# Attention followed by two MLP layers on one core: a third buffer for decoded weights, and the static instruction order drawn again

## The chip, the core and the metric

The kernel runs on one core of one Trainium2 chip. The metric is device time in microseconds (us) of one execution, the median of several runs. Five engines work side by side, each on its own queue in order: TensorE (PE, with its weight loads shown as PEld), VectorE (DVE), ScalarE (ACT), GpSimd (POOL) and SyncE (SP), which here only starts DMAs.

## What is computed

The reference, cut to what matters:

```python
# q, k, v: 4 batches, 8 heads, 576 positions, 64 wide
scores = q @ k.transpose(0, 1, 3, 2) / sqrt(64)
thresh = max(scores, axis=-1) - tau                 # tau = 0.02
scores = where(scores >= thresh, scores, -1e9)
attn   = exp(scores - max(scores));  attn /= sum(attn) + 1e-9
x      = (attn @ v) as 2304 tokens of 512
h  = x @ w_in;    x = (h * cos(h)) @ w_out          # 512 -> 2048 -> 512
h  = x @ w_in2;   out = (s * relu(h)**2 + b) @ w_out2
```

The weights arrive as 64-bit numbers, and the kernel decodes them to 32 bits itself.

## The kernel before

**Attention.** The work is cut into 16 pairs of heads (`pair(n)`), and a pair into nine tiles of 128 rows. A tile goes through: `scores` on PE (L312) into one of two PSUM tiles `s`; `stat` on DVE (L330), the row minimum `mn` of the negated scores; `limit` on POOL (the threshold `thr`); `expo` on ACT (L338, `e`); and `mask` on DVE (L342, `p`, with row sums), which also frees the `s` tile. `turn` (L271) transposes finished tiles on PE into PSUM tiles `pt`, and ACT copies them to `PT`. `weighted` (L425) multiplies with `v` in ten pieces for a pair (`av`), `finish` copies the result out on ACT, and `normalise` scales it on POOL.

**Layers.** 2304 tokens go through in five blocks for each of two layers, four of 512 tokens and one of 256. A block has 16 steps `f` (`step`; two at a time in the small block): `hidden` on PE (L651, 12 matmuls into `h`), an activation of five or seven instructions on DVE, ACT and POOL that ends with `gl` on POOL, and `output` on PE (L749, 12 matmuls into `acc`). The float32 factors are split in a high and a low part and multiplied in three products.

**Decoding.** Each layer has 32 half-weights: for each `f` a half of `w_in` and one of `w_out`. `decode` (L520) loads a raw tile `wr` by DMA (ring of two), then makes the word in a tile `wt` (ring of two): `magnitude` on ACT, `clamp` on POOL, `shift`, `sign` and `fill` on DVE (L545, L550, L555; `fill` frees `wr`), then `high` on ACT, or on POOL for the first 15 halves, and `low` on POOL, which frees `wt`. The first 15 halves of layer 1 have memory of their own and are decoded in the attention's time; the other 17 must wait until the attention's tiles are given up. Layer 2's halves take the places of layer 1's.

**The order.** Nothing of the order is left to a compiler. Class `Order` collects every operation with its engine, a planned length in ns, a rank, what it comes after, and the ring places that it takes and gives back. `run` (L80) plays the plan in planned time: on each engine it looks at the first 48 operations by rank, finds the one that could start first, and takes the lowest rank among those that could start within `SLACK` ns of it. `LAG`, 90 ns, is put between engines, and `tail` is time after an operation's end before its result counts. The operations are then issued in that order, and each engine keeps to it whatever the real times are. A rank is a place such as `base = n * PAIR` for pair n, `at = base + i * PAIR // 9` for tile i, or `close + step * STEP` in the layers, plus an offset from the table `PLACE`. Ranks only say which operation goes first; `PAIR` needn't be the time of a pair.

Of the kernel before, what the change touches and what calls it, by code (L numbers as in the profile page):

```python
# [27 lines left out]
class Order:  # L28
# [3 lines left out]

    SLACK = 262
    LAG = 90
    WINDOW = 48

# [12 lines left out]
    def add(self, engine, length, rank, fn, after=(), take=(), give=(), tail=0):  # L51
        op = dict(
            n=len(self.ops), engine=engine, length=length, rank=rank, fn=fn,
            after=[a for a in after if a is not None], take=tuple(take), give=tuple(give),
            tail=tail, start=None, end=None,
        )
        self.ops.append(op)
        return op
# [57 lines left out]
EARLY = 15  # L116

WEIGH = (3, 4)
PAIR = 16840

PLACE = {
    "scores": -6086, "stat": -3181, "exp": -7313, "mask": 1993, "turn": 1108, "turned": 3152, "rest": 443,
    "rested": -1757, "sums": 1929, "weigh0": -252, "weigh1": 4687, "weigh_step": 1086, "finish": -4708,
    "normalise": 40063, "keys": -30127, "early": 3.337, "early_step": 1.142, "first": 3.121, "second": 1.354,
    "second_step": 0.963, "first_step": 0.523, "xin": -10749, "active": 5021, "output": 5748,
}
STEP = 5450

# [2 lines left out]
def attention_moe_moe2_kernel(  # L131
# [33 lines left out]
    add, ring, ticket = order.add, order.ring, order.ticket  # L165
# [32 lines left out]

    for half in halves[:EARLY]:
        open_w(half)  # L200
    wtp = ctx.enter_context(tc.tile_pool(name="wtp", bufs=2))
    mg = ctx.enter_context(tc.tile_pool(name="mg", bufs=2))


# [13 lines left out]

    for name, size in (
        ("s", 2), ("pt", 4), ("q", 2), ("k", 1), ("ks", 2), ("v", 2), ("e", 2), ("p", 12), ("PT", 2),  # L220
        ("rb", 1), ("xs", 1), ("wr", 2), ("wt", 2), ("r", 2), ("gh", 2), ("gl", 2), ("mn", 6), ("thr", 6),
    ):
        ring(name, size)

# [3 lines left out]
    mixed = 4  # L228
# [4 lines left out]
    def pair(n):  # L233
# [3 lines left out]
        tk = {x: ticket(x) for x in ("q", "k", "ks", "v", "PT", "rb", "xs")}  # L237
# [18 lines left out]
        lk, lq, lv = load("k"), load("q"), load("v")  # L256
# [9 lines left out]
        ks = add("POOL" if n else "ACT", 700, base + PLACE["keys"], scale_keys, after=[lk], take=[tk["ks"]], give=[tk["k"]])  # L266
# [4 lines left out]
        def turn(tiles):  # L271
            if "PT" not in T:
                T["PT"] = apt.tile([P, 9, S], F32, tag="PT", name=f"PT{n}")
            pts = T["pt", tiles[0]] = [ps_t.tile([P, 512], F32, tag="pt", name=f"pt{n}_{tiles[0]}_{g}") for g in range(2)]
            for k in range(4):
                for j, i in enumerate(tiles):
                    p = T["p", i].rearrange("p a b -> p (a b)")
                    for g in range(2):
                        o = slice(64 * g, 64 * g + 64)
                        c = (k * len(tiles) + j) * 64  # L280
                        nc.tensor.transpose(pts[g][:, c : c + 64], p[o, k * 128 : k * 128 + 128], ident[o, o])  # L281
            if tiles[0] == mixed:
                p = T["p", mixed].rearrange("p a b -> p (a b)")
                nc.tensor.transpose(pts[0][0:64, 256:320], p[0:64, 512:S], ident[0:64, 0:64])
                nc.tensor.transpose(pts[1][:, 256:320], p[64:128, S - 128 : S], ident[64:128, 64:128])
# [16 lines left out]
        masks, scored, transposed = [], [], []  # L302
        ptk = []
        for i in range(9):
            for _ in range(WEIGH.count(i)):
                yield
            at = base + i * PAIR // 9
            heads = [0] if i < mixed else [1] if i > mixed else [0, 1]
            ts, te, tp, tm, th = ticket("s"), ticket("e"), ticket("p"), ticket("mn"), ticket("thr")
            ptk.append(tp)  # L310

            def scores(i=i):  # L312
                st = T["s", i] = ps_s.tile([P, 2, 512], F32, tag="s", name=f"s{n}_{i}")
                for h in range(2):
                    g = slice(64 * h, 64 * h + 64)
                    if i != mixed:
                        c, hd = columns[i], int(i > mixed)
                        nc.tensor.matmul(  # L318
                            st[:, h, :H2], T["q"][g, c : c + 128], T["ks"][g, hd * H2 : (hd + 1) * H2],
                            start=True, stop=True,  # L320
                        )
                        continue
                    for hd in range(2):
                        c = 512 + 64 * hd
                        nc.tensor.matmul(  # L325
                            st[64 * hd : 64 * hd + 64, h, :H2], T["q"][g, c : c + 64], T["ks"][g, hd * H2 : (hd + 1) * H2],
                            start=True, stop=True,
                        )

            def stat(i=i):  # L330
                T["mn", i] = atiny.tile([P, 1], F32, tag="mn", name=f"mn{n}_{i}")
                nc.vector.tensor_reduce(out=T["mn", i], in_=T["s", i][:, :, :H2], axis=mybir.AxisListType.XY, op=ALU.min)  # L332

            def limit(i=i):
                T["thr", i] = atiny.tile([P, 1], F32, tag="thr", name=f"thr{n}_{i}")
                nc.gpsimd.tensor_tensor(out=T["thr", i], in0=T["mn", i], in1=ptau, op=ALU.add)  # L336

            def expo(i=i):  # L338
                T["e", i] = ape.tile([P, 2, H2], F32, tag="e", name=f"e{n}_{i}")
                nc.scalar.activation(T["e", i], T["s", i][:, :, :H2], AF.Exp, bias=T["mn", i], scale=-1.0)  # L340

            def mask(i=i):  # L342
                if "sm" not in T:
                    tail_ops()
                p = T["p", i] = app.tile([P, 2, H2], F32, tag="p", name=f"p{n}_{i}")
                nc.vector.scalar_tensor_tensor(  # L346
                    out=p, in0=T["s", i][:, :, :H2], scalar=T["thr", i], in1=T["e", i], op0=ALU.is_le, op1=ALU.mult,
                    accum_out=T["sm"][:, i : i + 1],
                )

            s_ = add("PE", 600 if i == mixed else 500, at + PLACE["scores"], scores, after=[lq, ks] if i == 0 else [], take=[ts],
                     give=[tk["q"], tk["ks"]] if i == 8 else [], tail=250)
            scored.append(s_)
            m_ = add("DVE", 755, at + PLACE["stat"], stat, after=[s_], take=[tm])
            t_ = add("POOL", 190, at + PLACE["stat"], limit, after=[m_], take=[th])
            e_ = add("ACT", 735, at + PLACE["exp"], expo, after=[m_], take=[te], give=[tm])
            k_ = add("DVE", 890, at + PLACE["mask"], mask, after=[e_, t_], take=[tp], give=[ts, te, th])
            masks.append(k_)
            if i in (1, 3, 4, 6, 8):
                tiles = [i] if i == mixed else [i - 1, i]  # L360
                tt = [ticket("pt"), ticket("pt")]
                r_ = add("PE", 280 * len(tiles), at + PLACE["turn"], lambda t=tiles: turn(t), after=[masks[j] for j in tiles],
                         take=[*tt, *([tk["PT"]] if i == 1 else [])], tail=170)
                for g in (1, 0):
                    c_ = add("ACT", 170 + 215 * len(tiles), at + PLACE["turned"], lambda g=g, t=tiles: store_turned(g, t),
                             after=[r_], give=[tt[g]])
                    transposed.append(c_)
        end = base + PAIR

# [19 lines left out]
        r_ = add("PE", 650, end + PLACE["rest"], turn_rest, after=masks, take=tt, give=ptk, tail=170)  # L389
# [52 lines left out]
        for h in range(2):  # L442
            yield
            ts = ticket("pt")
            for k in range(5):
                v1 = add(
                    "PE", 490 + 100 * (k % 4 == 0), end + PLACE[f"weigh{h}"] + k * PLACE["weigh_step"], lambda h=h, k=k: weighted(h, k),
                    after=[*transposed, lv] if h == k == 0 else [v1], take=[ts] if k == 0 else [],
                    give=[tk["PT"], tk["v"]] if h * k == 4 else [],
                    tail=250 * (k == 4),  # L450
# [3 lines left out]
                take=[tk["xs"]] if h == 0 else [], give=[ts],  # L454
# [65 lines left out]
    def decode(half, rank, opened):  # L520
# [52 lines left out]
        early = opened is None  # L573
        o = add("SP", 60, rank - 6000, load, take=[tr], tail=4000)
        o = add("ACT", 675, rank, magnitude, after=[o], take=[tt])
        o = add("POOL", 620 if early else 720, rank, clamp, after=[o])
        o = add("DVE", 430 if early else 600, rank, shift, after=[o])
        o = add("DVE", 690 if early else 1030, rank, sign, after=[o])
        o = add("DVE", 690 if early else 1150, rank, fill, after=[o], give=[tr])
        o = add("POOL" if early else "ACT", 630, rank, high, after=[o, opened], take=[tw])  # L580
        o = add("POOL", 1270 if early else 1370, rank, low, after=[o], give=[tt])
# [302 lines left out]
```

## Time and profile before

| what | value |
|---|---|
| three runs | 1146.82, 1147.77, 1151.14 us; median 1147.77 us |
| profiled execution | 1150.11 us, its span 1148.3 us |
| PE busy | 1075.1 us (94% of the span) |
| DVE busy | 657.6 us (57%) |
| ACT busy | 483.7 us (42%) |
| POOL busy | 455.2 us (40%) |

The profiled execution is 2.3 us above the median, and its span leaves 1.8 us of it outside. The shares are means over stages with different limits: the attention up to some 313 us, layer 1 with decoding beside it, layer 1 alone, layer 1's end and layer 2's start with layer 2's decoding beside them, and layer 2 alone. [...]

### The profile page before, as it was taken

To read this page: it belongs to the slowest core of one execution; us is meant where nothing else is said; L and a number is where in the kernel's file an instruction comes from. 1 tells how busy PE (TensorE), PEld (TensorE's weight loads), DVE (VectorE), ACT (ScalarE), POOL (GpSimd) and SP (SyncE) were. 2 spreads that over 40 slices of the span, in tenths; PEclk is the share of its full clock that TensorE was granted. 3 is DMA by queue.
4 is the path that set the end of the run, shared out by engine and by line. 5 is a ranking of instruction groups with operands and counts; after the bars stand their busy time and mean duration, and the time that the engine had idled before them with its cause. 6 is when DMAs were issued, how large, how long until landed. Compare 5 with 4: busy or idle time off the path is not lost.

```text
span 1148.3 us, 17581 instructions
## 1 busy us (share of the span) xinstructions
PE 1075.1 (94%) x6736; PEld 816.2 (71%) x6736; DVE 657.6 (57%) x1062; ACT 483.7 (42%) x880; POOL 455.2 (40%) x556
## 2 busy tenths in 40 slices
PE   5988897889799889999999999999999999999998
PEld 3544444444467657889988877788888898888886
DVE  5778888788888864344553677887821222112211
ACT  4767776667644342222322343454422222223221
POOL 1133424233377744333333466676632222222222
PEclk9989999999899989999999999999999999999999
DMA  4232423232132211000010012333200000000100
GB/s 163 65 115 79 137 83 133 83 115 73 60 103 92 91 57 36 1 1 1 1 37 1 19 58 87 95 91 93 74 37 1 1 37 1 19 1 1 37 1 37
DMA packets 23507, 63.59 MB, mean 55 GB/s; under 512 B 4464, under 2 KB 4736, under 8 KB 23424
## 3 DMA queue, kind: packets, MB, share of 16 engines
q1 hardware_dynamic: 23280, 62.48, 16.8%
q8 instruction: 53, 0.87, 0.3%
q14 instruction: 30, 0.25, 0.1%
q10 hardware_dynamic: 144, 0.00, 0.0%
HBM read 57.67 MB, written 4.79 MB: 54 GB/s over the span
## 4 chain that ended last, share of the span: by engine, by line
PE 70%; DVE 14%; issue 7%; POOL 5%; ACT 2%; DMA 1%; POOLq 0%; DVEq 0%; ACTq 0%; SPq 0%
PE h L657 27%; PE acc L760 14%; PE acc L758 12%; PE s L318 7%; PE av L430 6%; DVE wt L550 3%; PE pt L281 2%; DVE p L346 2%; DVE wt L555 2%; DVE wt L545 2%; DVE mn L332 2%; DVE r L687 1%; POOL r L700 1%; PE s L325 1%; POOL wt L542 1%
## 5 line engine op out<-in xcount | busy, mean ns | idle before, releaser
L657 PE MATMUL h<-x,wh 128*128 128x512 f32 (+1 forms) x1280 | 371.2, 375 | 8.3 <-DVE r L708 6.3
L189 POOL TENSOR_TENSOR gl<-r,gh 128x512 fp32r<-128x512 f32 x144 | 190.8, 1325 | 306.5 <-DVE gh L731 242.1
L657 PEld LDWEIGHTS h<-x,wh 128*128 128x128 f32 x1280 | 232.3, 189 | 59.4 <-DVE r L708 9.4
L657 PE MATMUL h<-x,wl 128*128 128x512 f32 (+1 forms) x640 | 239.4, 374 | 0.3 <-POOL wl L189 0.3
L687 DVE TENSOR_SCALAR r<-r,s_t,b_t 128x512 f32<-128x512 f32 x72 | 44.0, 613 | 191.5 <-ACT r L226 191.5
L318 PE MATMUL s<-ks,q 64*128 64x288 f32 x512 | 108.4, 500 | 47.4 <-DVE p L346 35.0
L226 ACT ACTIVATE r<-h 128x512 f32<-128x512 f32 x72 | 43.2, 599 | 232.8 <-PE h L657 215.9
L657 PEld LDWEIGHTS h<-x,wl 128*128 128x128 f32 x640 | 120.8, 189 | 23.9 <-POOL wl L189 0.9
L332 DVE TENSOR_REDUCE mn<-s 128x1 f32<-128x576 f32 x144 | 108.9, 756 | 46.0 <-PE s L318 39.7
L340 ACT ACTIVATE e<-s,mn 128x576 f32<-128x576 f32 x144 | 106.5, 739 | 51.2 <-DVE mn L332 49.1
L346 DVE SCALAR_TENSOR_TENSOR p<-s,thr,e 128x576 f32<-128x576 f32 x144 | 116.2, 814 | 14.4 <-ACT e L340 10.0
L758 PE MATMUL acc<-gh,wh 128*128 128x512 f32 (+1 forms) x320 | 119.1, 372 | 4.0 <-ACT wh L568 4.0
L758 PE MATMUL acc<-gl,wh 128*128 128x512 f32 (+1 forms) x320 | 119.2, 372 | 2.6 <-POOL gl L189 2.6
L226 ACT ACTIVATE r<-r,hpi 128x512 f32<-128x512 f32 x72 | 51.9, 721 | 163.8 <-POOL r L700 163.6
L758 PE MATMUL acc<-gh,wl 128*128 128x512 f32 (+1 forms) x320 | 119.2, 372 | 0.1
L760 PE MATMUL acc<-wh,gl 128*128 128x512 f32 x288 | 112.6, 391 | 0.0
L760 PE MATMUL acc<-wl,gh 128*128 128x512 f32 x288 | 112.4, 390 | 0.0
L760 PE MATMUL acc<-wh,gh 128*128 128x512 f32 x288 | 112.3, 390 | 0.0
L318 PEld LDWEIGHTS s<-ks,q 64*128 64x128 f32 x512 | 45.8, 208 | 86.2 <-issue 52.4
L189 POOL TENSOR_TENSOR wl<-wt,wh 128x512 fp32r<-128x512 f32 x64 | 89.9, 1405 | 39.5 <-ACT wh L568 38.8
L336 POOL TENSOR_TENSOR thr<-mn,ptau 128x1 f32<-128x1 f32 x144 | 32.4, 227 | 176.5 <-DVE mn L332 170.8
L430 PE MATMUL av<-PT,v 128*64 128x288 f32 x640 | 96.2, 420 | 0.0
(64 smaller groups left out, 1436.5 us busy)
## 6 DMA issues: line engine op xcount, KB each, us to landing
wr<-in_w_dram SPq DMA_DIRECT2D x64, 512.0 KB, 3.6
q<-in_qt_dram SPq DMA_DIRECT2D x15, 576.0 KB, 3.8
v<-in_va_dram SPq DMA_DIRECT2D x16, 320.0 KB, 3.6
k<-in_kt_dram SPq DMA_DIRECT2D x16, 288.0 KB
out_dram<-ob SPq DMA_DIRECT2D x18, 256.0 KB, 2.2
rb<-rd SPq DMA_DIRECT2D x16, 144.0 KB, 3.4
rb<-rd SPq DMA_DIRECT2D x16, 128.0 KB, 3.1
q<-in_qt_dram SPq DMA_DIRECT2D x1, 448.0 KB
```

Of the source, the lines that this page charges most:

```text
L189: (eng or nc.gpsimd).tensor_tensor(out=o, in0=a, in1=b.bitcast(F32), op=ALU.subtract)
L226: nc.scalar.activation(o, x, fn, **kw)
L318: nc.tensor.matmul(st[:, h, :H2], T["q"][g, c : c + 128], T["ks"][g, hd * H2 : (hd + 1) * H2], start=True, stop=True,)
L332: nc.vector.tensor_reduce(out=T["mn", i], in_=T["s", i][:, :, :H2], axis=mybir.AxisListType.XY, op=ALU.min)
L340: nc.scalar.activation(T["e", i], T["s", i][:, :, :H2], AF.Exp, bias=T["mn", i], scale=-1.0)
L346: nc.vector.scalar_tensor_tensor(out=p, in0=T["s", i][:, :, :H2], scalar=T["thr", i], in1=T["e", i], op0=ALU.is_le, op1=ALU.mult, accum_ou ...
L430: nc.tensor.matmul(T["av", h][g, :H2], T["v"][:, hd, k, :], T["PT"][:, 4 if k == 4 else k + 5 * hd, h * H2 : (h + 1) * H2], start=(k == 0) ...
L550: nc.vector.scalar_tensor_tensor(out=T["t"], in0=T["raw"][:, :, 1], scalar=0x3FFFFFFF, in1=T["t"], op0=ALU.bitwise_or, op1=ALU.bitwise_and)
L657: nc.tensor.matmul(B["h"][:, e * n : (e + 1) * n], wt[:, c * P : (c + 1) * P], x, start=(c == 0 and j == 0), stop=(c == HP - 1 and j == 2),)
L687: nc.vector.tensor_scalar(out=o, in0=x, scalar1=s1, scalar2=s2_, op0=ALU.mult, op1=ALU.add)
L758: nc.tensor.matmul(acc[d][:, :n], wt[:, d * P : (d + 1) * P], g, **st)
L760: nc.tensor.matmul(acc[d], g[:, d * P : (d + 1) * P], wt, **st)
```

## The change

The pool and the ring for `wt` get a third tile. The planned lengths of the scores, the transposes and the late decoding on DVE are others, `SLACK` and `PAIR` are smaller, and the offsets in `PLACE` are others. No instruction is added or taken away; what each computes stays; the order in which engines issue them is another.

```diff
-    SLACK = 262
+    SLACK = 170
...
-PAIR = 16840
+PAIR = 11247
 PLACE = {
-    "scores": -6086, "stat": -3181, "exp": -7313, "mask": 1993, "turn": 1108, "turned": 3152, "rest": 443,
-    "rested": -1757, "sums": 1929, "weigh0": -252, "weigh1": 4687, "weigh_step": 1086, "finish": -4708,
-    "normalise": 40063, "keys": -30127, "early": 3.337, "early_step": 1.142, "first": 3.121, "second": 1.354,
-    "second_step": 0.963, "first_step": 0.523, "xin": -10749, "active": 5021, "output": 5748,
+    "scores": -6086, "stat": -7756, "exp": -5403, "mask": 1116, "turn": 1691, "turned": 3152, "rest": -417,
+    "rested": -956, "sums": 1929, "weigh0": -959, "weigh1": 4124, "weigh_step": 1387, "finish": -3724,
+    "normalise": 49805, "keys": -33243, "early": 3.071, "early_step": 1.0, "first": 4.196, "second": 0.936,
+    "second_step": 0.963, "first_step": 0.721, "xin": -6179, "active": 5880, "output": 1499,
 }
...
-    wtp = ctx.enter_context(tc.tile_pool(name="wtp", bufs=2))
+    wtp = ctx.enter_context(tc.tile_pool(name="wtp", bufs=3))
...
-        ("rb", 1), ("xs", 1), ("wr", 2), ("wt", 2), ("r", 2), ("gh", 2), ("gl", 2), ("mn", 6), ("thr", 6),
+        ("rb", 1), ("xs", 1), ("wr", 2), ("wt", 3), ("r", 2), ("gh", 2), ("gl", 2), ("mn", 6), ("thr", 6),
...
-            s_ = add("PE", 600 if i == mixed else 500, at + PLACE["scores"], scores, after=[lq, ks] if i == 0 else [], take=[ts],
-                     give=[tk["q"], tk["ks"]] if i == 8 else [], tail=250)
+            s_ = add("PE", 660 if i == mixed else 620, at + PLACE["scores"], scores, after=[lq, ks] if i == 0 else [], take=[ts],
+                     give=[tk["q"], tk["ks"]] if i == 8 else [], tail=130)
...
-                r_ = add("PE", 280 * len(tiles), at + PLACE["turn"], lambda t=tiles: turn(t), after=[masks[j] for j in tiles],
+                r_ = add("PE", 310 * len(tiles), at + PLACE["turn"], lambda t=tiles: turn(t), after=[masks[j] for j in tiles],
...
-        o = add("DVE", 430 if early else 600, rank, shift, after=[o])
-        o = add("DVE", 690 if early else 1030, rank, sign, after=[o])
+        o = add("DVE", 430 if early else 900, rank, shift, after=[o])
+        o = add("DVE", 690 if early else 1100, rank, sign, after=[o])
```

## Rows read from the trace of the kernel before

**Rows 1.** Busy time by engine in six stretches, then granted clock, DMA share, GB/s

```profile
20.00:300.00 280.00, 238.87 (x2739) 134.80 (x2739) 226.42 (x449) 193.14 (x395) 93.11 (x211) 0.95 0.30 97
300.00:320.00 20.00, 16.07 (x155) 10.45 (x152) 17.47 (x29) 11.10 (x25) 9.21 (x13) 0.83 0.27 76
320.00:440.00 120.00, 108.79 (x464) 82.85 (x464) 93.12 (x112) 48.53 (x79) 77.89 (x74) 0.97 0.27 85
440.00:640.00 200.00, 199.15 (x1050) 170.57 (x1049) 89.00 (x132) 54.57 (x92) 72.23 (x76) 1.00 0.02 6
640.00:826.00 186.00, 182.81 (x788) 147.03 (x787) 147.22 (x182) 84.67 (x141) 121.89 (x111) 1.00 0.26 80
826.00:1148.30 322.30, 318.12 (x1475) 263.29 (x1473) 74.00 (x141) 82.45 (x137) 78.12 (x60) 1.00 0.04 15
```

**Rows 2.** Waits, 0 to 300 us: us in total, times, longest

```profile
DVE mn L332 <- PE s L318: 38.7, 62, 2.2
PE s L318 <- DVE p L346: 35.0, 30, 2.6
DVE p L346 <- ACT e L340: 9.7, 38, 0.7
```

**Rows 3.** Instruction groups on DVE, 0 to 300 us: busy us, mean ns

```profile
L346 DVE SCALAR_TENSOR_TENSOR p<-s,thr,e 128x576 f32<-128x576 f32 x140 | 113.0, 814 | 13.9 <-ACT e L340 9.7 <-POOL thr L336 1.4
L332 DVE TENSOR_REDUCE mn<-s 128x1 f32<-128x576 f32 x140 | 105.9, 756 | 44.9 <-PE s L318 38.7 <-PE s L325 2.8
...
L346 DVE DVE_READ_ACCUMULATOR p<-s,thr,e 128x1 f32 x139 | 11.5, 83 | 0.0
L555 DVE SCALAR_TENSOR_TENSOR wt<-wr,wt 128x512 int32<-128x512 int32 x11 | 8.6, 786 | 0.0
L545 DVE TENSOR_SCALAR wt<-wt 128x512 int32<-128x512 int32 x12 | 7.6, 636 | 0.0
L550 DVE SCALAR_TENSOR_TENSOR wt<-wr,wt 128x512 int32<-128x512 int32 x11 | 7.6, 687 | 0.1
```

**Rows 4.** Timeline of PE in the attention: start us, duration us

```profile
169.68 0.76 PE L318 MATMUL s<-ks,q 64*128 64x288 f32 x4
170.37 0.71 PE L430 MATMUL av<-PT,v 128*64 128x288 f32 x4
171.00 0.76 PE L318 MATMUL s<-ks,q 64*128 64x288 f32 x4
```

**Rows 5.** Timeline of PE a few us later, idle time before in brackets

```profile
177.75 0.76 PE L318 MATMUL s<-ks,q 64*128 64x288 f32 x4 [2.51 <-DVE p L346]
...
179.08 1.32 PE L318 MATMUL s<-ks,q 64*128 64x288 f32 x4
```

**Rows 6.** Busy time by engine in the stretch right behind that wait

```profile
180.00:181.30 1.30, 1.30 (x34) 0.94 (x32) 0.86 (x3) 0.61 (x2) 0.02 (x1) 0.50 0.10 36
```

**Rows 7.** Instruction groups of the decoding on DVE, 300 to 440 us

```profile
L550 DVE SCALAR_TENSOR_TENSOR wt<-wr,wt 128x512 int32<-128x512 int32 x21 | 22.5, 1070 | 0.3
...
L545 DVE TENSOR_SCALAR wt<-wt 128x512 int32<-128x512 int32 x20 | 21.5, 1076 | 10.4 <-POOL wt L542 10.3
L555 DVE SCALAR_TENSOR_TENSOR wt<-wr,wt 128x512 int32<-128x512 int32 x21 | 20.2, 961 | 0.5
```

**Rows 8.** Waits, 300 to 440 us

```profile
ACT wt L538 <- POOL wl L189: 15.2, 8, 2.4
...
ACT wt L538 <- DMA wr<-in_w_dram: 8.2, 4, 3.0
```

**Rows 9.** The chain that ended last, at 402 us: start us, us

```profile
402.12 3.54 DMA wr<-in_w_dram
```

**Rows 10.** Timeline of POOL and DVE in the decoding: start us, duration us

```profile
387.42 1.30 POOL L189 TENSOR_TENSOR gl<-r,gh 128x512 fp32r<-128x512 f32 x1 [0.34 <-ACT gh L226]
387.46 1.54 DVE L545 TENSOR_SCALAR wt<-wt 128x512 int32<-128x512 int32 x1
...
406.19 0.42 DVE L545 TENSOR_SCALAR wt<-wt 128x512 int32<-128x512 int32 x1
```

## The prediction

> **What bounds the kernel now.** I read the page's shares first: PE is busy for 94% of the span, so all that an order can win lies in what is left, about 73 us, and in time at the lower clock. The second view, busy time by stretch, says where that is [rows 1]. From 20 to 300 us, in the attention, PE is idle for 41.1 us and DVE for 53.6, with the granted clock at 0.95. From 300 to 320 PE is idle for 3.9 us. From 320 to 440 us, where layer 1's first block runs beside the decoding of its later halves, PE is idle for 11.2 us. From 440 to 640 us it is 0.9 us, with layer 2's decoding 3.2 us, and over all of layer 2 alone 4.2 us, most of it the last output. So the two layers behind 440 us are PE's own work, in any order. Only the attention and the stretch behind it are open.
>
> The third view, waits in the first 300 us, says what PE and DVE wait for in the attention [rows 2]: each other. DVE stands 38.7 us, in 62 waits, for scores, and PE stands 35.0 us, in 30 waits, for a mask, which frees one of the only two score tiles. ACT is a small part of it, 9.7 us. Neither engine is full, yet neither can go on: the order in which the small pieces on PE stand between two score tiles decides.
>
> DVE is the fuller of the two. A tile costs it 0.756 for the minimum, 0.814 for the mask and 0.083 us for the read of the sum, 1.653 us [rows 3]. With 144 tiles that is 238 us, with fourteen early halves at 2.11 us (0.636, 0.687 and 0.786) 268 us. The attention takes some 300 us from its first tile to its last. So 32 us is the most that any order can win there.
>
> **Part by part: the planned scores.** The plan gives PE 0.50 us for a score tile, then the next piece may start. In the trace the next piece starts 0.69 us behind a score tile (169.68 to 170.37), and a score tile 0.63 us behind a piece of `av` (170.37 to 171.00) [rows 4]. Each score tile thus puts what is planned behind it 0.19 us late, and these delays add up until PE runs empty. The new plan says 0.62 us, and so takes 0.12 of the 0.19 away. The time until the result counts (length with `tail`, 0.75 us) stays. I put down 0.12 us for each of the 62 waits: 7.4 us less. Bounds: nothing, if another piece then stands in the way, and 32 us, if the new order packs DVE fully. I stay near the low end, because the nearest row, the 0.19 us, is a third of a mean wait (38.7 by 62, 0.62 us). The transposes' new length has the same sign and lies in these bounds.
>
> **The offsets in the attention.** In tiles (`PAIR` by nine: 1871 ns before, 1250 after) the pieces of `av` stand 1.11 tiles apart and no longer 0.58, so they are spread over more of the pair. Against that, the minimum's rank moves to 6.2 tiles ahead of its tile's place, where it stood 1.7, and the mask's from 1.07 behind to 0.9 behind. DVE will more often take the next minimum before a mask. I count nothing for both together; the loss that they can bring is the rival below.
>
> **Early halves.** Half j has rank 3.337 + 1.142 j pairs before and 3.071 + j after. Up to 16 pairs that is twelve halves before (j = 11 at 15.90), and thirteen after, with the next at 16.07. I count two more in the attention; one is the other bound. They cost DVE there 2 x 2.11 = 4.2 us [rows 3]. DVE's idle 53.6 us covers them only when they fall into its waits for scores; I put down half, 2.1 us more, with 0 and 4.2 as bounds.
>
> Behind the attention the same two halves are missing, and there a half costs DVE 1.076 + 1.070 + 0.961 = 3.11 us [rows 7]. DVE is busy for 93.1 of 120 us [rows 1], two thirds of it decoding (21 halves, 64 us), and the chain there runs over DVE and POOL. So two halves less are 6.2 us less. This fits into PE's idle 11.2 us; those with the clock (0.03 of 120 us, 3.6 us) make 14.8 us the upper bound, nothing the lower one: the late halves' ranks also move back, from 3.121 + 0.523 j steps to 4.196 + 0.721 j, and may give it back.
>
> **The third tile.** In this stretch ACT waits 15.2 us, eight times, for `wl` to free a word tile, and 8.2 us, four times, for a raw tile to land [rows 8]. The raw ring stays at two. A raw tile is loaded only when `fill` has freed one, and the load takes 3.54 us until it lands; just this load, not a word tile, stands on the chain that ended last at 402 us [rows 9]. So next behind the wait removed is the load, and ACT isn't what DVE waits for most. I count nothing, within the upper bound of the same 14.8 us. In layer 2's decoding it can win 3.2 us at most, PE's idle there; nothing as well.
>
> DVE's `shift` takes 1.54 us when POOL's `gl` starts beside it and 0.42 us when it has the time to itself [rows 10]. [...]
>
> What a late `shift` costs is in the rows without any rule: if all 17 late halves met POOL, their mean of 1.08 us would become 1.54, and DVE would lose 17 x 0.46 = 7.8 us.
>
> **Outputs, activation and the smaller slack.** `output` moves from 3.05 to 2.28 steps behind its step, so one `hidden` less stands between. Beyond 440 us PE's queue has idle time of 0.9 us in 200 [rows 1], and all of the activation's engines have more than half of their time free, so I count nothing. A smaller `SLACK` makes the plan take the operation that can start first a little more often; it has no row, and lies in the attention's bounds. SP has no work moved past a transfer that PE waits for, but for the raw load, which is counted.
>
> **The sum.** 1150.1 us is the profiled execution. Less 7.4 (scores), more 2.1 (early halves in the attention), less 6.2 (the same halves later): 11.5 us less, 1138.6 us. The profile lies 2.3 us above the median, so for the median of 1147.8 it is 1136.3, and I say 1136 us.
>
> **The rivals.** *Slower: minima before masks.* A mask frees a score tile, a minimum doesn't. If DVE takes a minimum or a piece of decoding first, PE runs empty. [...] Such waits now cost 35.0 by 30, 1.17 us each [rows 2]; with 1.30 us at half clock 1.8. One more for each pair is 16 x 1.17 to 1.8, 19 to 29 us. With 4.1 us won by the halves (6.2 less 2.1) and nothing by the scores: 1163 to 1173 us. It becomes slower than the bound of 5.7 us from (4.1 + 5.7) by 1.17, eight more waits in the whole attention, one in two pairs. For it speaks the minimum's rank; against it that the two score tiles limit how far minima can run ahead, and that the plan knows of this ring.
>
> [...]
>
> *Much faster.* The order packs DVE: 32 us in the attention and 6.2 behind it, 1110 us. Against it: at 0.95 granted clock PE is itself near its limit, 238.9 of 280 us.
>
> **How the numbers follow.** 0.5% of this time, 5.7 us, is about what a measurement can tell from no change. I give 0.50 to the forecast (1123 to 1142 us; 25 to 5.7 us less), 0.08 to much faster (below 1123), 0.24 to no change, with 0.07 of it by the port's rule, and 0.18 to slower. Faster is 0.58, same 0.24, slower 0.18. The range goes from 1117 us, which leaves out half of much faster, to 1158 us, between no change and the slower rival's 1163, which leaves out most of that one: some 0.16 in all.
>
> **What would show it.** In the profile after: DVE's waits for scores in the attention below 38.7 us, near 31, and PE's for masks no longer than 35; thirteen or fourteen `fill` instructions done before the layers start; PE idle by 5 us or less in the 120 us behind, with no stretch at 0.50 in it; ACT's waits for a word tile gone, and those for `wr` longer. From 440 us on all should look as before. The forecast is wrong if waits of PE for masks grow by eight or more, if the granted clock in the attention falls below 0.95, or if the late halves, ranked further back, make `output` wait at the end of the first block for longer than now.

## The result and the profile after

The changed kernel takes 1106.8 us (median of 4 runs, 1105.7 to 1109.5) against 1149.4 us for the kernel before (the three runs above and a fourth): a ratio of 0.963, 95% interval 0.9595 to 0.9665, 43 us less. The forecast was 1136 us and its range ended at 1117 us: the sign was right, the size was not.

Busy time by stretch of the kernel after, with stretches moved by the 20 us by which the layers start sooner. As in [rows 1], a line has the stretch and its us, the busy us and instructions of PE, PEld, DVE, ACT and POOL, the granted clock (TensorE's, as a share of its full clock), the DMA share and GB/s.

```profile
20.00:280.00 260.00, 223.47 (x2702) 130.15 (x2698) 223.61 (x450) 192.15 (x393) 102.46 (x218) 0.99 0.34 109
...
300.00:420.00 120.00, 118.11 (x522) 92.99 (x517) 98.94 (x121) 52.47 (x83) 81.40 (x77) 1.00 0.26 78
420.00:620.00 200.00, 200.00 (x1054) 171.45 (x1054) 88.61 (x133) 59.25 (x94) 72.85 (x77) 1.00 0.03 9
620.00:806.00 186.00, 185.15 (x804) 150.59 (x804) 147.91 (x183) 85.88 (x141) 124.04 (x109) 1.00 0.26 82
```

The idle time of PE behind the attention is gone (1.9 of 120 us, before 11.2), DVE in the attention is busier (86% for 81%), and the granted clock in the attention is 0.99 for 0.95. Two points of time in each trace cut the span: the start of the first `hidden`, and the first copy of layer 1's first block out of `acc`. Before they lie at 313.8 and 440.7 us, after at 293.7 and 401.2. So the attention got shorter by 20.1 us, the first block by 19.4 (126.9 to 107.5), and all that follows by 1.1 (707.6 to 706.5). (The expectation for e1 puts the first `hidden` of the kernel after at 294.4 us, so its 19.4 and 20.1 stand the other way round.)

Waits in the attention, 0 to 294 us of the kernel after:

```profile
PE s L318 <- DVE p L346: 26.1, 25, 1.7
DVE mn L332 <- PE s L318: 23.4, 52, 2.2
DVE p L346 <- ACT e L340: 14.1, 58, 0.5
```

DVE's waits for scores fell from 38.7 to 23.4 us [rows 2], twice as far as I had said. PE's waits for masks fell too, from 35.0 to 26.1.

**Where the attention's time came from.** DVE takes two minima, then two masks, in all 72 cycles of both traces. What differs most is how soon PE starts the next scores when a mask has freed a tile. Timeline of the kernel before, PE and DVE:

```profile
152.22 2.16 PE L430 MATMUL av<-PT,v 128*64 128x288 f32 x16
...
152.71 0.82 DVE L346 SCALAR_TENSOR_TENSOR p<-s,thr,e 128x576 f32<-128x576 f32 x1
...
154.31 0.76 PE L318 MATMUL s<-ks,q 64*128 64x288 f32 x4
...
155.11 1.60 DVE L332 TENSOR_REDUCE mn<-s 128x1 f32<-128x576 f32 x2 [0.63 <-PE s L318]
```

The mask is done at 153.53 us, but four pieces of `av` are under way, the scores start 0.78 us later, and DVE stands 0.63 us. The kernel after:

```profile
140.53 0.82 DVE L346 SCALAR_TENSOR_TENSOR p<-s,thr,e 128x576 f32<-128x576 f32 x1
140.57 1.19 PE L430 MATMUL av<-PT,v 128*64 128x288 f32 x8
...
141.69 0.76 PE L318 MATMUL s<-ks,q 64*128 64x288 f32 x4
```

Here two pieces stand in between, and the scores start 0.34 us behind the mask (141.35). From the starts and ends of tiles 20 to 129 the mean of this delay is 0.56 us before and 0.33 after; delays over 1 us are 20 before and 2 after. With two score tiles, the time from one mask's end to the end of the mask two tiles on is two tiles' time. Before, its five parts are 0.56 (delay) + 0.88 (scores to minimum) + 0.76 (minimum) + 1.16 (to the mask) + 0.81 (mask), 4.17 us or 2.085 a tile. After they are 0.33, 0.94, 0.75, 1.12 and 0.81, 3.95 us. The starts of scores give 2.086 and 1.974 us a tile. The parts cut up the tile's time and don't by themselves say what caused what, but the delay is the only one that fell by more than 0.05 us. Of the 20.1 us, 12.3 lie between tiles 20 and 130 and most of the others behind them.

The delay alone isn't the price. In e15, below, it is 0.52 us and a tile takes 2.007. In e8 it is 0.45 and a tile takes 2.107, since there the time from the minimum to the mask grew to 1.30 us. That a late score tile costs DVE its idle time is seen directly (0.63 us in the first timeline above); that every part of the gain went this way isn't shown.

**Where the first block's time came from.** The block of the kernel before, and of the kernel after:

```profile
313.80:440.70 126.90, 115.69 (x515) 88.19 (x514) 99.10 (x119) 50.03 (x82) 81.94 (x78) 0.96 0.27 86
```

```profile
293.70:401.20 107.50, 105.39 (x498) 81.69 (x495) 94.00 (x114) 51.70 (x86) 75.01 (x72) 1.00 0.29 87
```

PE's idle time fell from 11.2 to 2.1 us, 9.1 of the 19.4. The other 10.3 us are less busy time, at a clock of 1.00 in place of 0.96 and with 17 instructions fewer within the block. PE hardly stops any more, which the 20 us stretches show (kernel after):

```profile
340.00:360.00 20.00, 20.00 (x89) 16.26 (x88) 18.22 (x23) 9.60 (x16) 14.55 (x15) 1.00 0.27 80
360.00:380.00 20.00, 20.00 (x89) 16.23 (x88) 19.20 (x23) 9.11 (x15) 15.53 (x16) 1.00 0.34 104
380.00:400.00 20.00, 18.11 (x75) 13.54 (x74) 16.71 (x20) 8.76 (x15) 10.82 (x11) 1.00 0.27 79
```

Fifteen halves are decoded when the layers start, before twelve.

### The profile page after: what moved, and what is told of

It is laid out like the page before. It is cut to its first block, busy times and chain, and to the rows that moved or that the text cites. A ratio compares the mean times of both kernels' runs of the same rounds, so it can differ in the third digit from the quotient of the medians.

```text
span 1107.7 us, 17596 instructions
## 1 busy us (share of the span) xinstructions
PE 1054.5 (95%) x6736; PEld 810.5 (73%) x6736; DVE 648.5 (59%) x1062; ACT 489.3 (44%) x880; POOL 459.5 (41%) x556
## 4 chain that ended last, share of the span: by engine, by line
PE 85%; DVE 9%; issue 2%; ACT 2%; POOL 1%; DMA 0%; DVEq 0%; ACTq 0%; POOLq 0%
PE h L657 35%; PE acc L760 18%; PE acc L758 16%; PE av L430 7%; PE s L318 6%; DVE mn L332 3%; DVE p L346 3%; PE pt L281 2%; PE s L325 1%; DVE wt L550 1%; ACT e L340 1%; POOL wl L189 1%; DVE wt L545 1%; DVE wt L555 1%; POOL gl L189 0%
## 5 line engine op out<-in xcount | busy, mean ns | idle before, releaser
L687 DVE TENSOR_SCALAR r<-r,s_t,b_t 128x512 f32<-128x512 f32 x72 | 40.3, 560 | 201.5 <-ACT r L226 201.3
L318 PE MATMUL s<-ks,q 64*128 64x288 f32 x512 | 99.0, 472 | 40.9 <-DVE p L346 26.1
L346 DVE SCALAR_TENSOR_TENSOR p<-s,thr,e 128x576 f32<-128x576 f32 x144 | 115.9, 811 | 15.1 <-ACT e L340 14.1
L332 DVE TENSOR_REDUCE mn<-s 128x1 f32<-128x576 f32 x144 | 107.6, 754 | 28.2 <-PE s L318 23.4
L189 POOL TENSOR_TENSOR wl<-wt,wh 128x512 fp32r<-128x512 f32 x64 | 85.2, 1332 | 51.0 <-ACT wh L568 46.2
L336 POOL TENSOR_TENSOR thr<-mn,ptau 128x1 f32<-128x1 f32 x144 | 38.6, 268 | 136.1 <-DVE mn L332 132.4
```

The costliest lines, as they stand in the source:

```text
L189: (eng or nc.gpsimd).tensor_tensor(out=o, in0=a, in1=b.bitcast(F32), op=ALU.subtract)
L318: nc.tensor.matmul(st[:, h, :H2], T["q"][g, c : c + 128], T["ks"][g, hd * H2 : (hd + 1) * H2], start=True, stop=True,)
L346: nc.vector.scalar_tensor_tensor(out=p, in0=T["s", i][:, :, :H2], scalar=T["thr", i], in1=T["e", i], op0=ALU.is_le, op1=ALU.mult, accum_ou ...
L687: nc.vector.tensor_scalar(out=o, in0=x, scalar1=s1, scalar2=s2_, op0=ALU.mult, op1=ALU.add)
```

## The experiments

Times are medians in us, ratios against the kernel before on the same chip with their 95% interval. The other columns come from the one profiled execution of each kernel, which need not be the median one. "First hidden" is the attention's length, "block" is the first block of layer 1, "rest" all behind it (span less the block's end), "tile" the time for a tile from the starts of scores, tiles 20 to 130. Runs e1 to e4, e5 to e8, e9 to e12, e13 to e16 and e17 to e18 shared a chip each. The kernel before took 1147.7 to 1150.7 us on them, so differences of a few us between chips say little. Diffs are shortened to the lines or values that changed.

| run | time | ratio | first hidden | block | rest | tile |
|---|---|---|---|---|---|---|
| before | 1149.4 | 1 | 313.8 | 126.9 | 707.6 | 2.086 |
| after | 1106.8 | 0.963 (0.9595 to 0.9665) | 293.7 | 107.5 | 706.5 | 1.974 |
| e1 | 1148.9 | 1.002 (1.0003 to 1.0037) | 312.8 | 126.2 | 707.6 | 2.096 |
| e2 | 1144.3 | 0.9956 (0.9935 to 0.9976) | 311.8 | 122.3 | 708.4 | 2.095 |
| e3 | 1145.8 | 0.9977 (0.9958 to 0.9996) | 312.5 | 125.0 | 707.6 | 2.139 |
| e4 | 1118.2 | 0.9743 (0.972 to 0.9766) | 291.7 | 115.4 | 709.3 | 1.957 |
| e5 | 1134.6 | 0.9864 (0.9845 to 0.9884) | 310.2 | 114.6 | 705.8 | 2.106 |
| e6 | 1133.2 | 0.9851 (0.9836 to 0.9865) | 291.7 | 125.5 | 715.1 | 1.957 |
| e7 | 1108.9 | 0.9646 (0.9628 to 0.9664) | 292.9 | 107.4 | 706.8 | 1.959 |
| e8 | 1132.5 | 0.985 (0.9834 to 0.9867) | 308.5 | 113.4 | 706.0 | 2.107 |
| e9 | 1122.0 | 0.9752 (0.971 to 0.9793) | 293.1 | 122.1 | 705.8 | 1.963 |
| e10 | 1122.2 | 0.9768 (0.9739 to 0.9797) | 291.9 | 121.2 | 706.3 | 1.975 |
| e11 | 1136.4 | 0.989 (0.986 to 0.9921) | 305.9 | 120.3 | 709.4 | 2.083 |
| e12 | 1151.7 | 1.0025 (1.0006 to 1.0043) | 315.9 | 126.5 | 709.2 | 2.088 |
| e13 | 1148.4 | 0.9995 (0.9971 to 1.0019) | 317.6 | 119.3 | 709.5 | 2.133 |
| e14 | 1131.2 | 0.9832 (0.9809 to 0.9855) | 299.2 | 124.6 | 710.1 | 2.036 |
| e15 | 1111.4 | 0.9664 (0.9645 to 0.9683) | 297.2 | 107.8 | 706.5 | 2.007 |
| e16 | 1113.6 | 0.9687 (0.9673 to 0.9702) | 291.3 | 115.9 | 705.9 | 1.957 |
| e17 | 1120.4 | 0.9749 (0.9717 to 0.9782) | 290.7 | 121.9 | 705.7 | 1.957 |
| e18 | 1112.7 | 0.9691 (0.9672 to 0.9709) | 293.3 | 113.1 | 705.7 | 1.974 |

**e1, the third tile alone on the kernel before.**

```diff
-tc.tile_pool(name="wtp", bufs=2) ... ("wt", 2)
+tc.tile_pool(name="wtp", bufs=3) ... ("wt", 3)
```

> The kernel before with the third word tile (pool and ring) and nothing else of the change. Between before and after, the attention up to the first hidden lost 19.4 us (313.8 to 294.4), the first block of layer 1 behind it 20.1 us (126.9 to 106.8), all that follows 1.1 us. Theory O (the order, by lengths and offsets, made both; the tile alone is idle, since the raw ring of two comes next): 1144 to 1150 us, first block 122 to 127 us. Rival T (the third tile made the first block's 20 us): about 1130 us, first block 107 to 110 us, attention as before.

Nothing, as theory O had it: by its interval the time is not shorter at all.

**e2, the lengths alone on the kernel before.**

```diff
-600 / 500, tail=250; 280 a tile; shift 600, sign 1030
+660 / 620, tail=130; 310 a tile; shift 900, sign 1100
```

> The kernel before with the new planned lengths of scores, transposes and decoding only; SLACK, PAIR, PLACE and two word tiles as before. Theory L (true lengths were what was missing): the attention loses 10 to 19 us, first hidden near 297 us, time 1125 to 1135 us. Rival P (the offsets do it, lengths by themselves only shuffle the order): first hidden within 5 us of 314, time 1143 to 1155 us.

The attention moved by 2 us: theory L falls, as far as it means lengths by themselves.

**e3, the offsets alone on the kernel before.** The diff's lines of `SLACK`, `PAIR` and `PLACE`.

> The kernel before with the new SLACK, PAIR and PLACE only; lengths and two word tiles as before. Theory P (offsets): first hidden at 295 to 300 us, time 1110 to 1125 us, with most of the first block won too. Rival L (lengths): the offsets were drawn for other lengths, so no gain, 1145 us or more.

2 us: theory P falls as well. Fifteen early halves are done in this run too, and the block is only 1.9 us shorter.

**e4, the changed kernel with two word tiles.** The diff of e1 backwards. This is also e2 and e3 together.

> The changed kernel with two word tiles, all else kept (so the order is drawn again with a ring of two). Theory O: 1107 to 1112 us, first block within 4 us of 106.8. Rival T: the first block goes back to 120 us or more, 1120 to 1127 us, attention stays at 294.

Lengths and offsets, 4 and 2 us apart, give 30 us together, and all of the attention. The block, 115.4 us, lies between the two theories' values. The tile gives 11 us on top by the medians; by the two traces it is 8.7 us, 7.9 less in the block and 2.8 less behind it against 2.0 more in the attention. PE in e4, 20 us stretches:

```profile
360.00:380.00 20.00, 18.04 (x76) 13.50 (x74) 18.46 (x21) 8.88 (x14) 13.90 (x14) 1.00 0.28 88
380.00:400.00 20.00, 16.32 (x60) 12.21 (x61) 13.46 (x18) 8.01 (x13) 9.05 (x10) 0.91 0.21 70
```

PE is idle here for 5.6 us, in the kernel after for 1.9. The granted clock of the second stretch is 0.91, in the kernel after 1.00.

**e5, the changed kernel with the old lengths on PE.**

```diff
-660 / 620, tail=130; 310 a tile
+600 / 500, tail=250; 280 a tile
```

> The changed kernel with the old planned lengths on PE (scores 500 and 600 with tail 250, transposes 280 a tile); new decoding lengths, offsets, SLACK and three tiles kept. So far offsets alone gave 2 us and lengths alone 4, but both with two tiles 30. Theory L (the offsets pay only in a plan that knows how long PE's pieces are): the attention loses its gain, first hidden at 308 us or later, 1122 to 1132 us. Rival D (it is the decoding's lengths that the offsets need): 1107 to 1113 us, first hidden near 294.

Theory L in its second form holds for the attention: 16.5 of its 20.1 us are gone. The time is above theory L's 1132 us, because the block also takes 7.1 us more. I had not foreseen that: the lengths put back are those of the attention's scores and transposes.

**e6, the changed kernel with the old decoding lengths.**

```diff
-shift 900, sign 1100
+shift 600, sign 1030
```

> The changed kernel with the old planned lengths of the late decoding (shift 600, sign 1030). Theory L: the attention stays at 294 us, as late halves aren't in it; the first block gets 2 to 8 us longer, 1108 to 1115 us. Rival D: 1120 us or more.

The attention stays, but the block takes 18 us more and the rest 8.6 more; the size is that of rival D. The chain of e6 through the block, start us and us (pieces below 0.1 us left out), is one cycle repeated:

```profile
343.58 0.57 issue
344.15 1.54 DVE wt L545
345.71 1.67 DVE wt L550
347.38 0.61 DVE r L687
348.02 0.70 DVE r L697
348.76 0.11 issue
348.87 0.92 POOL r L700
349.82 0.73 ACT r L226
350.61 0.57 issue
```

POOL's work beside them, from the timeline:

```profile
344.11 1.28 POOL L189 TENSOR_TENSOR wl<-wt,wh 128x512 fp32r<-128x512 f32 x1 [0.66 <-ACT wh L568]
345.35 1.49 POOL L189 TENSOR_TENSOR gl<-r,gh 128x512 fp32r<-128x512 f32 x1
```

The cycle comes again at 350.61, so a step takes 7.03 us. ("issue" is time without a wait that the profile shows; by the timeline DVE ran the activation's last instruction, L708, in each 0.57 us.) PE finishes its share of a step sooner and is then idle, 3.2 and 4.0 us in two stretches of 20:

```profile
340.00:360.00 20.00, 16.80 (x71) 12.88 (x70) 16.00 (x19) 6.96 (x11) 11.87 (x12) 1.00 0.26 79
360.00:380.00 20.00, 16.01 (x67) 11.85 (x65) 16.04 (x18) 7.50 (x12) 11.67 (x12) 1.00 0.24 71
```

The order puts `shift` beside POOL's `wl` and `sign` beside its `gl`, between two steps' activations, and they take 1.54 and 1.67 us.

**e7, the changed kernel with minima and masks ranked as before in tiles.**

```diff
-"stat": -7756, "mask": 1116
+"stat": -2125, "mask": 1332
```

> The changed kernel with the ranks of the minimum and the mask put back to where they stood in tiles before (stat -2125, mask 1332: 1.7 tiles ahead and 1.07 behind). Rival S of the prediction (minima taken before masks make PE run empty): faster than the changed kernel, 1095 to 1104 us, fewer waits of PE for masks. Theory M (early minima keep ACT and DVE fed and are part of the gain): first hidden 3 to 15 us later, 1110 to 1122 us. No effect (the two score tiles decide it): within 3 us of 1107.

No effect beyond the noise: in the changed kernel their rank decides nothing.

**e8, the changed kernel with `av` ranked as before in tiles.**

```diff
-"weigh0": -959, "weigh1": 4124, "weigh_step": 1387
+"weigh0": -168, "weigh1": 3130, "weigh_step": 725
```

> The changed kernel with the ten pieces of av ranked as before in tiles (0.58 tiles apart; weigh0 -168, weigh1 3130, weigh_step 725). Theory W (the spread of these pieces keeps PE fed and its clock up): granted clock in the attention falls from 0.99 towards 0.95, first hidden 5 to 15 us later, 1112 to 1122 us. Rival: the plan puts them where PE is free whatever their rank; within 4 us of 1107.

Theory W holds for the attention: 14.8 us, within its 5 to 15, and a granted clock of 0.95 from 20 to 290 us. The time is 10 us above theory W's 1122, 5.9 of them from the block. No run has the spread alone on the kernel before. Waits of e8, 0 to 310 us:

```profile
DVE mn L332 <- PE s L318: 33.2, 71, 2.2
PE s L318 <- DVE p L346: 32.8, 37, 2.2
```

**e9, e17 and e18, the changed kernel with the old ranks of the decoding:** of both kinds (e9), of the early halves (e17), of the late ones (e18).

```diff
-"early": 3.071, "early_step": 1.0, "first": 4.196, "first_step": 0.721
+"early": 3.337, "early_step": 1.142, "first": 3.121, "first_step": 0.523
```

> The changed kernel with the old ranks of the decoding in layer 1 (early 3.337 and 1.142, first 3.121 and 0.523): fewer halves in the attention, the late ones ranked sooner. The prediction put 6.2 us on two early halves and up to 4.2 us against them in the attention. Theory E (early halves are a large part of the first block's 20 us): attention 0 to 4 us shorter, first block 8 to 16 us longer, 1112 to 1120 us. Rival F (the fit of planned to real decoding lengths and the third tile make the block, ranks matter little): within 4 us of 1107.

> The changed kernel with the ranks of the early halves alone put back (3.337 and 1.142). With these and the late ranks put back together (e9) 13 early halves were done when the layers started, and the first block took 122 us in place of 107. Theory: it was the early halves (17 left become 19): first block 114 to 122 us, 1115 to 1123 us. Rival: it was the late ranks; within 4 us of 1107.

> The changed kernel with the ranks of the late halves alone put back (3.121 and 0.523 steps, so sooner among the steps' activations). Theory of the early halves: within 4 us of 1107. Rival (decoding ranked ahead of activations makes PE wait in the first block): first block 114 to 122 us, 1115 to 1123 us.

With 13 early halves done in place of 15 the block takes 14.4 us more and the attention 3.0 less (e17). With the late ranks back the block takes 5.6 us more (e18), between the two values expected. The block of e9 takes 14.6 us more, as theory E had it, and isn't the sum of the two; its time is 2 us above theory E's.

**e10, the changed kernel with `SLACK` at 262.**

> The changed kernel with SLACK back at 262. Theory: the plan's choices change in many places, but lengths, spread and decoding stay, so attention and first block each within 4 us, 1104 to 1113 us. Rival (the drawn order is a lucky draw which any change of a choice loses): 1120 us or more.

My theory falls, and the time is the lucky draw's: 1122 us. The attention is as good, but 13 halves are done when the layers start, though their ranks are those of the changed kernel, and the block takes 13.7 us more. The choices moved where nobody had aimed.

**e11 and e14, PE's lengths and the spread of `av` on the kernel before,** e14 with the transposes' and three other offsets as well.

```diff
+660 / 620, tail=130; 310 a tile; "weigh0": -1436, "weigh1": 6175, "weigh_step": 2077
+e14: "turn": 2532, "rest": -624, "rested": -1431, "exp": -8090, "finish": -5576
```

> The kernel before with two things of the change alone: the new planned lengths on PE (scores, transposes), and the pieces of av ranked as far apart in tiles as after (weigh0 -1436, weigh1 6175, weigh_step 2077 at PAIR 16840). Undoing either cost the whole gain in the attention. If both together are enough: first hidden at 294 to 300 us, granted clock near 0.99, first block as before or a little changed, 1126 to 1136 us. If other offsets are needed too: first hidden within 5 us of 312, 1140 us or more.

> The kernel before with the new planned lengths on PE, the spread of av, and also the changed offsets of the transposes, of their copies, of the exponentials and of finish, in tiles or pairs as after (turn 2532, rest -624, rested -1431, exp -8090, finish -5576 at PAIR 16840). Without these last five the first hidden came at 305.9 us. Theory T (later transposes leave PE free when a score tile is freed): first hidden 292 to 299 us, 1122 to 1130 us. Rival (what is missing lies in PAIR, SLACK or the early halves): first hidden 303 us or later, 1133 us or more.

7.9 us of the attention's 20.1 with the first, between the two values expected; 14.6 with the second, at the end of theory T's range. What makes the remainder wasn't tested. The granted clock from 20 to 290 us is 0.95 in e11 and 0.96 in e14, against 0.95 before, so these microseconds came with hardly any of the clock's rise.

**e15, the changed kernel with the transposes ranked back.**

```diff
-"turn": 1691, "rest": -417, "rested": -956
+"turn": 740, "rest": 296, "rested": -1173
```

> The changed kernel with the transposes and their last copies ranked as before in tiles (turn 740, rest 296, rested -1173). Theory T: the time from a mask's end to the next scores grows from 0.33 towards 0.5 us, first hidden 4 to 14 us later, 1111 to 1122 us. Rival (their rank matters as little as that of the minima): within 4 us of 1107.

The delay behind a mask grows to 0.52 us, as theory T had it, but the time from the minimum to the mask shrinks to 1.06, and the attention takes only 3.5 us more. A small part.

**e12, decoding lengths and third tile on the kernel before.** The diffs of e1 and of e6 (backwards).

> The kernel before with the new decoding lengths and the third word tile alone. Undoing the lengths cost the first block 18 us, undoing the tile 8 us, both of 20. If both together are enough: attention as before (first hidden 310 to 315), first block 106 to 113 us, 1128 to 1136 us. If the early halves or the late ranks are needed too: first block 118 to 124 us, 1138 to 1146 us.

Neither value: the block stays at 126.5 us. Taking either out of the changed kernel costs the block 7.9 or 18 us, and both together do nothing here.

**e13, all early halves in the attention of the kernel before.**

```diff
-"early": 3.337, "early_step": 1.142
+"early": 2.0, "early_step": 0.95
```

> The kernel before with the ranks of the early halves alone changed (early 2.0, early_step 0.95 pairs), so that all fifteen rank inside the attention; two tiles, old lengths, all else as before. In the runs so far the first block ends 3 to 5 us behind the last half's decoding, and takes 6.0 to 6.2 us for each half that isn't decoded when the layers start (before 20 left, 126.9 us; after 17 left, 106.8 us). Theory H (a half costs the block a whole turn of some 6.1 us): 17 left, first block 107 to 112 us; attention 0 to 6 us longer for three more halves; 1128 to 1139 us. Rival (a half costs what DVE spends on it, 3.11 us, as the prediction had it): first block 116 to 119 us, 1140 to 1146 us.

My theory H falls. Fifteen halves are done, the block gets 7.6 us shorter, near the rival's 9.3, and the attention gets 3.8 longer, the rest 1.9. The time, 1148.4 us, is above both expected ranges.

**e16, three raw tiles in the changed kernel, and 14 early halves.**

```diff
-EARLY = 15 ... name="small", bufs=2 ... ("wr", 2)
+EARLY = 14 ... name="small", bufs=3 ... ("wr", 3)
```

> The changed kernel with a third raw tile (pool and ring wr), paid for with the memory of the fifteenth early half (EARLY 14), so 18 halves are left to the first block. In the changed kernel ACT waits 27 us for raw tiles to land. Theory R (the load is what holds a half's turn at 6.05 us): a turn falls to 5.0 to 5.6 us, first block 94 to 105 us, 1095 to 1105 us. Rival (DVE, POOL and their meetings hold it): 18 halves at 6.05 us, first block 112 to 114 us, 1112 to 1116 us.

Theory R falls. The block's 115.9 us are 8.4 more than after, about what one half more costs by e17 (7.2), and the time is in the rival's range. ACT's waits for raw tiles, 294 to 440 us, the kernel after first and e16 behind it:

```profile
ACT wt L538 <- DMA wr<-in_w_dram: 27.1, 13, 2.5
```

```profile
ACT wt L538 <- DMA wr<-in_w_dram: 9.6, 8, 1.8
```

The waits shrink and the block doesn't. No run was faster than the changed kernel.

**The runs together.** The attention is robust: in the eight runs e4, e6, e7, e9, e10 and e16 to e18, each with an order drawn anew, it takes 290.7 to 293.3 us, and only in e5, e8 and, by 3.5 us, e15 does it get longer. So its gain doesn't hang on one lucky draw. The block isn't robust: in nine of the eleven runs that alter one part of the changed kernel (e4 to e10 and e15 to e18) it gets 5.6 to 18 us longer, e5 and e8 among them, which alter operations of the attention. So the size of one part's loss in the block can't be told from that of a new draw.

## Why the prediction was wrong, step by step

*What bounds the kernel* held: all but 1.1 us of the 40.6 us in the spans came out of the attention and the block behind it.

Three terms failed: the scores, the attention's offsets, and the third tile. I had 5.3 us less in the attention (7.4 less 2.1) and 6.2 in the block; 20.1 and 19.4 were measured.

*The planned scores* (7.4 us) were mis-sized, and the way of counting was wrong. I gave each wait the lateness of one piece. In fact the lengths win 2 us of the attention by themselves (e2), and without PE's lengths the changed kernel loses 16.5 of 20.1 us (e5). What a true length buys isn't its own 0.12 us in 62 waits; with the offsets a tile takes 0.112 us less over all tiles measured, and the delay behind a mask falls from 0.56 to 0.33 us.

*The offsets in the attention*, counted as nothing, failed outright: without the spread of `av`, which I described and then priced at zero, the changed kernel loses 14.8 us (e8). The loss set against it, minima before masks, isn't there: DVE's cycle is the same in both traces, and their rank changes nothing (e7). The slower rival rested on it; its 1.8 us are the 1.17 us of a wait [rows 2] and half of the 1.30 us for which [rows 6] shows a granted clock of 0.50.

*The early halves* (6.2 us less in the block, 2.1 more in the attention) had the right direction and the wrong size: three more and not two. In the attention two cost 3.0 us (e17), within my bounds. In the block e17 gives 14.4 us for two, 7.2 us a half where I had 3.11. Three halves more in the attention came with a block shorter by 7.6 us in e13, 2.5 a half, and by 1.9 in e3, 0.6 a half. So a half has no price of its own, and DVE's time isn't it. My upper bound for the stretch, 14.8 us, was broken as well: it left out 313.8 to 320 us, where the block already ran and [rows 1] shows a clock of 0.83.

*The third tile* (nothing) failed: 11 us in the changed kernel (e4, 8.7 by the traces), nothing on the kernel before (e1). I read the raw load as next in line [rows 9]; in e16 a third raw tile cut the waits for it from 27.1 to 9.6 us, and the block was no shorter than one more half explains. The waits I named went as said: for word tiles to none, for raw tiles from 8.2 to 27.1 us.

*`shift` beside POOL* is real, but its 7.8 us did not come: in the changed kernel the 17 late ones take 0.90 us in the mean, where it was 1.08 [rows 7]. In e6 their mean is 1.12 us, 1.38 for the twelve from 320 to 400 us, and `shift` and `sign` beside POOL, 1.54 and 1.67 us, set the step. No run shows the port's rule, by which I gave 0.07 to no change; what the runs show in its place are these times, 1.54 us for `shift` beside POOL and 0.42 us by itself [rows 10]. In e6 the drawn order puts them on the chain, with 7.03 us a step.

*Much faster* (1110 us, 0.08) came nearest. That its sum, 38 us, is close to the 40.6 of the traces is luck, because it had 32 us in the attention and 6.2 behind it where 20.1 and 19.4 were measured. Its objection, PE near its limit at 0.95 clock, took the granted clock as given; it rose to 0.99 with the better order. How much of the attention's 20 us is the clock itself no run separates. e14 won 14.6 us of them at 0.96 from 20 to 290 us, and e7, at 0.97, is as fast there as the changed kernel at 0.99, which speaks for a small part.

Open: why decoding lengths and tile do nothing on the old offsets (e12), what each part of the change gives to the first block apart from the draw, and which offsets make up the last 5.5 us of e14's attention.

## What to carry to other kernels

With a static order drawn from planned lengths, measure the lengths first and draw the offsets anew on them: apart they gave 4 and 2 us here, together 30. Find the loop that goes through the scarcest buffer, here the two score tiles, and ask of each piece on the engine that refills it whether it can stand in the way when the buffer comes free. Don't price such a change by adding up parts: undoing the tile, the decoding's lengths, the early ranks or `SLACK` lost 8 to 18 us each of the first block's 19, while on the kernel before the tile won 0.7 us there, all the lengths 4.6 (e2), and ranks that bring fifteen early halves 7.6 (e13). And change something that should not matter: where the time moves all the same, as in the block with e5, e8 and e10, the draw itself is part of what was measured.

## What the hardware showed that I had not expected

That `shift` on DVE takes 0.42 us by itself and 1.54 us beside POOL I had seen [rows 10]; in the first block of the kernel before `sign` and `fill`, too, go from 0.68 to 1.67 us. In e6 an order that repeats the meeting in every step holds PE to a step of 7.03 us, which costs PE 3.2 and 4.0 us of two stretches of 20. The granted clock went with the order, too: its mean in the attention (20 to 290 us) was 0.92 to 0.95 in the kernel before, e1 to e3, e8 and e11 to e13, 0.96 in e5 and e14, and 0.97 to 1.00 in all that kept the changed kernel's lengths on PE and its spread of `av`.
